# The last integer shift of the vector engine's exponential tiles moves to GpSimd, with a new tile table

## The chip, the cores and the metric

The program runs on one core of one Trainium2 chip. A core has five engines, each with an instruction queue of its own that it works off strictly in order: TensorE (PE in the profile; its weight loads are shown as PEld), VectorE (DVE), ScalarE (ACT), GpSimd (POOL) and SyncE (SP, which here only issues DMAs). They share the on-chip memory SBUF; TensorE writes its products to PSUM, eight banks of 512 float32 columns by 128 partitions. The engines wait for one another through semaphores. The metric is the device time of one execution in microseconds (us).

## The reference

One transformer block in parallel form on x of shape 1 x 2048 x 512 in bf16: the layer-normed input goes through attention and through a feed-forward part, and both are added to x.

```python
def _A_ref(x, wq, wk, wv, wo):                 # 32 query heads of 16, one shared key/value head
    ...
    scores = jnp.einsum("bhqd,bkd->bhqk", q, k) * (Dh ** -0.5)
    p = _softmax(scores, axis=-1)
    o = jnp.einsum("bhqk,bkd->bhqd", p, v)
    ...
def _B_ref(x, w1, b1, w2, b2):                 # 512 -> 1792 -> 512
    h = _gelu(jnp.einsum("bsd,df->bsf", x, w1) + b1)
    return jnp.einsum("bsf,fd->bsd", h, w2) + b2
xn = _layernorm(x, axis=-1)
return x + _A_ref(xn, A_wq, A_wk, A_wv, A_wo) + _B_ref(xn, B_w1, B_b1, B_w2, B_b2)
```

The softmax has 32 x 2048 x 2048 exponentials, some 134 million. They are what the kernel is built around.

## The kernel before

**Tiles and units.** The exponentials are cut into 2048 tiles of 128 keys by 512 queries of one head. Four heads make a group, a group has 64 tiles, and there are 32 groups (8 per block of 512 queries, four blocks). Three tiles in a row form a unit; there are 683 units. `scores(u)` (L890) makes the scores of a unit with three matmuls of 32 rows each into three PSUM banks. Two sets of three banks take turns, so the scores of unit u+2 can only be written when everything of unit u has been read out of its banks.

**Two ways to an exponential.** A table, the string `DTAB`, has one character per unit and says which of its tiles are E tiles and which are D tiles.

- The E tiles of a unit are done by one activation on ScalarE, `exp(u)` (L913), PSUM to the SBUF tile `E`. Each needs one product with V.
- A D tile is done on VectorE. `p1` (L944) reads the scores from PSUM, adds an offset, clamps from below and writes int16 into `Dt`: read as the bits of a bf16 this is a straight-line approximation of the exponential. To mend it, five copies of the tile are used, shifted by -26, 0, 26, 51 and 77 (`SPL_K`); each is multiplied with a copy of V scaled by a weight of its own (`SPL_C`), and TensorE sums the five products. A D tile therefore needs five products with V (`pv_mm`, L949), an E tile one.

**Batches and shifts.** D tiles are gathered into batches of one to six (a character of `CLOSE` ends a batch). `close_batch` makes the shifted copies on VectorE, SBUF to SBUF in int16 (L977), with the three steps of `SPL_STEPS`, each given as destination buffer, source buffer, number of buffers, constant:

```python
SPL_STEPS = ((1, 0, 1, 26), (2, 0, 2, 51), (0, 0, 1, -26))
```

The first writes buffer 1 from buffer 0; the second writes buffers 2 and 3 from buffers 0 and 1 in one instruction; the third shifts buffer 0 in place, when the product with the unshifted tile and both earlier steps have read it. So a batch of n tiles takes three instructions, over n, 2n and n tiles, and the products that use each copy become ready behind it.

**The rest.** VectorE also evacuates the products' sums (`o_evac`, L989), normalises them (L1016, both inputs in SBUF), moves the results of the side matmuls out of PSUM (L1052, L1065, L1080, L1126) and squares the queries (L1053, both inputs in SBUF). ScalarE also runs the GELU (L1092). TensorE runs, between the scores and the products with V, all side matmuls (projections, feed-forward; `mm4`, L605). GpSimd has only the set-up: constants, masks and the scaled copies of V (L847), all within the first 29 us.

**Order.** The instruction order of every engine is written before the program is emitted, by `Prog.schedule`. It plays the program through with a cost (`occ`) and a latency (`lat`) for each operation and gives each engine, when it becomes free, the ready operation with the earliest due time (`rdy + allow`; `P1_ALLOW = -20` puts a ready `p1` ahead of all else on VectorE). `emit` then writes each engine's list with the semaphore waits that the dependences need. At run time nothing is reordered.

Of the kernel before, what the change touches and what calls it, by code (L numbers as in the profile page):

```python
# [15 lines left out]
SPL_K = (-26, 0, 26, 51, 77)  # L16
SPL_C = (0.39453125, 0.349609375, 0.298828125, 0.259765625, 0.2265625)
SPL_NB = 4
SPL_STEPS = ((1, 0, 1, 26), (2, 0, 2, 51), (0, 0, 1, -26))
SPL_D = -107.78043958019079  # L20
SPL_MIN = 64.0
SWITCH = 0.1
# [10 lines left out]
EV_ALLOW = -2.0  # L33
# [10 lines left out]
LAL = 30.0  # L44
LCO = 0.0
PRO_FROM = 2.0
TBL = 1
DMASK = {".": (), "0": (0,), "2": (2,), "a": (0, 1), "b": (1, 2), "x": (0, 1, 2),
         "o": (0,), "t": (2,), "A": (0, 1), "B": (1, 2), "X": (0, 1, 2)}
CLOSE = "otABX"  # L50
DTAB = "t00o0.202.oot.0.ot2b...2ot20.20.t.o222200...o20t.202.2o.2o.2.o0220.o0o...t22o0.ot2..22t..00t0o2t.0.0t2022..0.0t2oa.222o.....o2to2o.2.2o.ott2.222t.20...00o00..oo.020oo.222oo.2to.aBxAoo22ot2.2..o.t0to2t22toot..200oo02...to.2ttt02t0000..00..222ot0t0.2.02o222.222.oo.o.22tt0t0.o..o002..2to002.t202.t.2tt0.002o0.0o.to.o.tt2...2.tot0202o20.o0..2..202o2.22o.02o..00o00.20t2A..2o22tt.2.22.0o.0.20.t2tt002.2t0.o0..2.t022.ot2.t.t2222t.0.22t0o2.0t222t...2ottt2..2t0to0.o0t..t2.to..00o2.2t.2o0o2.2..0.o..2o..o.to2.o0.02toXxxA.22t2.2t2.000o20.02.2t.2o2a..t2.t0t.00o00222.o0t0t.o22222t2.00..2.0o.2ot.o22.t2o.t.20o2t220t2...022ott020...t2.0o00.2o20.20o2.t.o2t22to.o..o222t.02022.200too..20t..2ooo.."
Y_ALLOW = 8.0
H_ALLOW = 5.0
YT_ALLOW = (3,3,3,3)
# [31 lines left out]

class _Op:
    __slots__ = ("eng", "fn", "deps", "sdeps", "stream", "amt", "need", "ticket", "waits", "clock", "occ", "lat",
                 "allow", "kind", "tag", "nun", "outs", "rel", "pm", "rdy", "start", "end", "vis", "idx", "done", "due", "real")


class Prog:
# [16 lines left out]
        self.fill_deps = []  # L109
        self.log = []  # L110

    def add(self, eng, fn, r=(), w=(), acc=None, dma=None, occ=0.1, lat=0.15, allow=1.0, kind=None, tag=None, after=(), due=None):
        op = _Op()
        op.eng, op.fn = eng, fn
        op.stream = dma or eng
        op.amt = 16 if dma else 1
# [89 lines left out]
    def schedule(self):  # L206
# [30 lines left out]
        opened = None  # L237
        s_seen = False
        vleft = sum(op.kind == "v" for op in ops)
        left = sum(1 for o in ops)  # L240
        nfill = 0
        while left:
# [11 lines left out]
            if e == "pe":  # L254
# [53 lines left out]
                if op is None or isinstance(op, float):  # L308
                    free["pe"] = t + 0.03 if op is None else op
                    continue  # L310
                visit = visit + 1 if op.kind in ("pv", "side") and mode == "col" else 1
            else:
                op = min(cand, key=self.due)
                if e == "dve" and op.kind != "p1":
                    nx = min([o.rdy for o in ready[e] if o.kind == "p1"] + [t + 9.0])
                    if 1e-6 < nx - t < min(P_WAIT, op.occ / 2):
                        free["dve"] = nx
                        continue
# [39 lines left out]
            else:  # L358
                op.start = t
                op.end = t + op.occ  # L360
                op.vis = op.end + op.lat
            if e == "pe":
                while op.start > wend:
                    slow = 1.0 if area > HAM_T * WIN else 2.0
                    ncold += slow > 1
                    self.log.append((wend - WIN, area / WIN, slow))
                    area, wend = 0.0, wend + WIN
                pend = op.start + op.occ * slow
# [52 lines left out]
    def emit(self):  # L421
# [4 lines left out]
        for op in self.ops:  # L426
            kn = known[op.eng]
            op.waits = []
            for o in sorted(op.deps, key=lambda o: -len(o.clock)):
                if kn.get(o.stream, 0) >= o.ticket:  # L430
                    continue
                op.waits.append((o.real, o.stream, o.ticket))
                for s, t in o.clock.items():
                    if kn.get(s, 0) < t:
                        kn[s] = t
# [31 lines left out]
def bass_parallel_sum__grouped_kv_mqa__dense_activation_gelu__prompt_kernel(  # L467
# [34 lines left out]
    with ExitStack() as es:  # L502
# [81 lines left out]
        def vcost(n, mode=1):  # L584
            return n / 0.96e3 / mode + 0.065
# [368 lines left out]
        def close_batch():  # L954
# [19 lines left out]
            for o, i, nb, k in SPL_STEPS:  # L974
                def keys(b):
                    return [(("D", base[b + m > 0] + q), b + m) for m in range(nb) for q in range(n)]
                dve(lambda e, d=view(o, nb), q=view(i, nb), k=k: e.tensor_scalar(d, q, float(k), None, ALU.add),  # L977
                    r=keys(i) if i != o else (), w=keys(o), n=nb * n * TBW, mode=4, allow=1.0, kind="post")
# [8 lines left out]
        def o_evac(gg):  # L987
# [59 lines left out]
        def q_pack(tb, p, gls=(0, 1)):  # L1047
            s = p % 2
            for d in range(DT):
# [233 lines left out]
```

## Time and profile before

| | |
|---|---|
| time, median of 3 runs | 767.58 us (767.33 to 769.11) |
| span of the profiled execution, first to last instruction | 765.7 us |
| busy: PE / DVE / ACT / POOL | 747.8 / 751.4 / 750.6 / 16.5 us |
| exponentials on ScalarE (L913) | 679 instructions, 699.8 us busy: 184 of three tiles, 487 of two, 8 of one |
| `p1` on VectorE (L944) | 498 instructions for 514 tiles, 339.9 us busy |
| shifts on VectorE (L977) | 663 instructions (221 batches), 348.5 us busy |
| products with V (L949) | 2570 of D tiles, 1534 of E tiles |

The time around the span (start and end of the execution) is not in the profile; the median of the three runs stands 1.9 us above the span of the profiled execution, whose own time is not given apart from it. The duration of a VectorE or ScalarE instruction in a row is longer than the distance to the start of the next one when two follow each other without a wait: the next starts before the last one's results have landed. Costs below are therefore distances from start to start of neighbours in the timeline, where they can be had.

### The profile page before, as it was taken

The page shows a single profiled execution, that of the slowest core. Times are in us where ns is not written, and L with a number is a line of the kernel's source. Part 1 is how long each engine was busy: PE and PEld are TensorE (multiplying, and loading weights), DVE is VectorE, ACT ScalarE, POOL GpSimd, SP SyncE. Part 2 cuts the span into 40 slices and gives each one's busy share as a digit, 9 for nine tenths or more (in the row PEclk, how much of TensorE's full clock was granted, in tenths as well). Part 3 has the DMA queues.
Part 4 walks back from the last instruction along what each step waited for, and adds up shares of the span by engine and source line. Part 5 has one row for each costly group of instructions (what it writes and reads, how often), then busy time and mean ns, then how long its engine had stood idle before and what let it go on. Part 6 is the DMA issues. An engine that isn't in the chain of part 4 may idle for free.

```text
span 765.7 us, 21236 instructions
## 1 busy us (share of the span) xinstructions
PE 747.8 (98%) x8948; PEld 231.4 (30%) x8950; DVE 751.4 (98%) x1403; ACT 750.6 (98%) x745; POOL 16.5 (2%) x55
## 2 busy tenths in 40 slices
PE   7999999999999999999999999999999999999998
PEld 5323222332232322222232223232233233322223
DVE  8899999999999999999999999999999999999997
ACT  8999999999999999999999999999999999999995
POOL 5300000000000000000000000000000000000000
PEclk8999999999999999999999999999999999999999
DMA  9100101000001010101100010100100101010001
GB/s 314 55 14 12 29 16 24 11 19 16 12 17 37 5 42 23 24 23 25 27 11 25 26 26 23 31 9 20 30 13 13 27 30 37 16 45 17 21 17 37
DMA packets 32072, 23.29 MB, mean 30 GB/s; under 512 B 16369, under 2 KB 27498, under 8 KB 31978
## 3 DMA queue, kind: packets, MB, share of 16 engines
q1 hardware_dynamic: 30922, 21.90, 11.1%
q8 instruction: 71, 1.16, 0.7%
q14 instruction: 23, 0.19, 0.1%
q10 hardware_dynamic: 1056, 0.03, 0.1%
HBM read 13.08 MB, written 2.35 MB: 20 GB/s over the span
## 4 chain that ended last, share of the span: by engine, by line
PE 42%; ACT 41%; DVE 14%; issue 1%; DMA 1%; DVEq 0%; SPq 0%; POOL 0%
ACT E L913 40%; PE pAll L949 20%; PE pAll L890 13%; PE pAll L605 8%; DVE Dt L944 6%; DVE Dt L977 6%; DVE x_sb L1080 1%; DMA x_sb<-in_A_x_dram 1%; PE pAll L599 1%; PE pAll L743 0%; DVE Of L989 0%; ACT xnT L748 0%; DVE ub L1080 0%; DVE qp L1052 0%; DVE stats L692 0%
## 5 line engine op out<-in xcount | busy, mean ns | idle before, releaser
L913 ACT ACTIVATE E<-pAll 128x1024 bf16<-128x1024 f32 (+1 forms) x679 | 699.8, 1272 | 1.4 <-PE pAll L890 0.5
L949 PE MATMUL pAll<-Dt,V 128*32 128x512 bf16 x2570 | 400.0, 384 | 1.0 <-DVE Of L989 0.7
L977 DVE TENSOR_SCALAR Dt<-Dt 128x1024 int16<-128x1024 int16 (+7 forms) x663 | 348.5, 559 | 0.6
L944 DVE TENSOR_SCALAR Dt<-pAll 128x512 int16<-128x512 f32 (+2 forms) x498 | 339.9, 695 | 1.7 <-PE pAll L890 1.3
L949 PE MATMUL pAll<-E,V 128*32 128x512 bf16 x1534 | 284.4, 385 | 0.5 <-DVE Of L989 0.3
L890 PE MATMUL pAll<-QT,KT 32*128 32x512 bf16 x2048 | 267.2, 384 | 5.0 <-ACT E L913 2.0
L890 PEld LDWEIGHTS pAll<-QT,KT 32*128 32x128 bf16 x2048 | 66.8, 91 | 279.5 <-ACT E L913 250.7
L949 PEld LDWEIGHTS pAll<-Dt,V 128*32 128x32 bf16 x2570 | 105.5, 94 | 120.2 <-issue 69.8
L605 PE MATMUL pAll<-xnT,w_sb 128*32 128x512 bf16 x896 | 113.2, 382 | 1.4 <-DVE x_sb L1080 1.1
L949 PEld LDWEIGHTS pAll<-E,V 128*32 128x32 bf16 x1534 | 67.5, 94 | 58.4 <-issue 43.0
L605 PE MATMUL pAll<-w_sb,x_sb 128*32 128x512 bf16 x448 | 74.0, 382 | 0.0
L605 PE MATMUL pAll<-w_sb,ub 128*32 128x512 bf16 x448 | 66.2, 382 | 0.0
L605 PE MATMUL pAll<-wop,oTp 128*32 128x512 bf16 x256 | 55.5, 382 | 0.0
L605 PEld LDWEIGHTS pAll<-xnT,w_sb 128*32 128x32 bf16 x896 | 29.5, 95 | 23.9 <-issue 9.1
L605 PE MATMUL pAll<-xnT,wq_sb 128*32 128x512 bf16 x256 | 21.1, 384 | 0.0
L989 DVE COPY Of<-pAll 128x512 f32<-128x512 f32 x31 | 21.0, 678 | 0.0
L1080 DVE TENSOR_SCALAR x_sb<-pAll,b1T 128x512 bf16<-128x512 f32 x28 | 20.7, 740 | 0.1
L1080 DVE TENSOR_SCALAR ub<-pAll,b1T 128x512 bf16<-128x512 f32 x28 | 20.7, 738 | 0.1
L605 PEld LDWEIGHTS pAll<-w_sb,x_sb 128*32 128x32 bf16 x448 | 18.4, 95 | 6.7 <-issue 4.5
L1244 PE MATMUL pAll<-xnT,zeros 128*32 128x512 bf16 x204 | 19.3, 382 | 0.0
L605 PE MATMUL pAll<-b2row,ones 128*32 128x512 bf16 x64 | 18.8, 382 | 0.0
L605 PEld LDWEIGHTS pAll<-w_sb,ub 128*32 128x32 bf16 x448 | 16.9, 94 | 5.9 <-issue 4.1
(118 smaller groups left out, 227.4 us busy)
## 6 DMA issues: line engine op xcount, KB each, us to landing
OfP<-Of SPq DMA_DIRECT2D x124, 32.0 KB, 2.0
rbP<-rden_rows SPq DMA_DIRECT2D x124, 32.0 KB, 1.9
w_sb<-in_B_w_dram SPq DMA_DIRECT2D x2, 1792.0 KB, 12.7
x_sb<-in_A_x_dram SPq DMA_DIRECT2D x8, 256.0 KB, 4.8
x_sb<-in_A_x_dram SPq DMA_DIRECT2D x16, 128.0 KB, 2.1
QT<-qp SPq DMA_DIRECT2D x124, 16.0 KB, 1.8
out_dram<-x_sb SPq DMA_DIRECT2D x12, 128.0 KB, 1.8
wq_sb<-in_A_wq_dram SPq DMA_DIRECT2D x1, 512.0 KB, 6.6
```

The source lines that it names most:

```text
L599: return add("pe", lambda e: e.matmul(o, l, rh, start=start, stop=stop, **kw), r, w, occ=occ, lat=0.23, allow=allow, **ak)
L605: add("pe", lambda e, c=c, j=j: e.matmul(o[c, :], l[:, c], rh, start=start, stop=stop, tile_position=(0, 32 * j)), r, [(k, j) for k in w] ...
L890: ins = e.matmul(o, l, rh, start=True, stop=True, tile_position=(q0, 0))
L913: o = act(lambda e: e.activation(E[:, s0:s0 + na, :], bank(b0, na).rearrange("p (a n) -> p a n", a=na), ACT.Exp, scale=LN2 / 128.0), w=[B( ...
L944: return dve(lambda e: e.tensor_scalar(Dt[:, s:s + n, :], bank(bk, n).rearrange("p (a n) -> p a n", a=n), float(127 * 128) + SPL_D, SPL_MI ...
L949: add("pe", lambda e, a, b: e.matmul(pO[32 * j:32 * j + 32, :], V1[:, v, kt, :], rhs, start=a, stop=b, tile_position=(0, 32 * j)), r=r + [ ...
L977: dve(lambda e, d=view(o, nb), q=view(i, nb), k=k: e.tensor_scalar(d, q, float(k), None, ALU.add), r=keys(i) if i != o else (), w=keys(o), ...
L989: dve(lambda e: e.tensor_copy(Of[:, i, :], pO), w=["O", ("Of", i)], allow=0.0)
L1080: dve(lambda e: e.tensor_scalar(ubs[tb % 2][:, ft, :], pM, b1T[:, ft:ft + 1], None, ALU.add), r=["b1T"], w=M4 + [ukey(tb, ft)], n=TBW + 57 ...
L1244: pr.filler = lambda e, j, o: e.matmul((pO if o else pM)[32 * j:32 * j + 32, :], zeros[:, 0:32], xnT[:, 0, 0:TBW], start=not o, stop=not o ...
```

## The change

- `SPL_STEPS` loses its third step. In its place `close_batch` adds, for each tile of the batch, one instruction on GpSimd that works on the tile in place: `tensor_scalar` with two operations, times 1.0 and plus -26.0. The product with that copy follows each tile's own instruction. Nothing of the arithmetic changes.
- The planner is told that a GpSimd shift takes 0.55 us and is seen 0.2 us later (`GS_OCC`, `GS_LAT`), and that it excludes VectorE's SBUF work: operations marked `two=True` (the shifts, L1016, L1053) don't start while a GpSimd shift runs (`lock`), and a GpSimd shift doesn't start while one of them runs, nor in the last 0.35 us of another VectorE operation (`GS_MIN`).
- So that the order holds at run time, each GpSimd shift also waits for the VectorE operation that stands ahead of the last marked one (`gate`). It may then be issued while that marked one still runs.
- A GpSimd shift that has been ready for 1 us (`GS_LATE`) while VectorE is free and no `p1` is ready is offered to VectorE, as a shift of one tile.
- `DTAB` is replaced. What the two tables hold, counted with the rules of `DMASK` and `CLOSE`:

| | before | after |
|---|---|---|
| D tiles | 514 | 539 |
| E tiles | 1534 | 1509 |
| batches | 221 | 276 |
| batches of 1 / 2 / 3 / 4 / 5 / 6 tiles | 80 / 58 / 40 / 22 / 16 / 5 | 133 / 70 / 42 / 20 / 6 / 5 |
| units with 0 / 1 / 2 / 3 D tiles | 185 / 486 / 8 / 4 | 188 / 458 / 30 / 7 |

```diff
--- before.py
+++ after.py
@@ -16,7 +16,8 @@
 SPL_K = (-26, 0, 26, 51, 77)
 SPL_C = (0.39453125, 0.349609375, 0.298828125, 0.259765625, 0.2265625)
 SPL_NB = 4
-SPL_STEPS = ((1, 0, 1, 26), (2, 0, 2, 51), (0, 0, 1, -26))
+SPL_STEPS = ((1, 0, 1, 26), (2, 0, 2, 51))
+SPL_LAST = -26.0
 SPL_D = -107.78043958019079
 SPL_MIN = 64.0
 SWITCH = 0.1
@@ -44,11 +45,16 @@
 LAL = 30.0
 LCO = 0.0
 PRO_FROM = 2.0
+GS_OCC = 0.55
+GS_LAT = 0.2
+GS_MIN = 0.35
+GS_LATE = 1.0
+GS_DUE = 1.0
 TBL = 1
 DMASK = {".": (), "0": (0,), "2": (2,), "a": (0, 1), "b": (1, 2), "x": (0, 1, 2),
          "o": (0,), "t": (2,), "A": (0, 1), "B": (1, 2), "X": (0, 1, 2)}
 CLOSE = "otABX"
-DTAB = "t00..."
+DTAB = "ot...."
 Y_ALLOW = 8.0
 H_ALLOW = 5.0
 YT_ALLOW = (3,3,3,3)
@@ -86,7 +92,8 @@
 
 class _Op:
     __slots__ = ("eng", "fn", "deps", "sdeps", "stream", "amt", "need", "ticket", "waits", "clock", "occ", "lat",
-                 "allow", "kind", "tag", "nun", "outs", "rel", "pm", "rdy", "start", "end", "vis", "idx", "done", "due", "real")
+                 "allow", "kind", "tag", "nun", "outs", "rel", "pm", "rdy", "start", "end", "vis", "idx", "done", "due", "real",
+                 "two", "alt", "gate")
 
 
 class Prog:
@@ -109,8 +116,10 @@
         self.fill_deps = []
         self.log = []
 
-    def add(self, eng, fn, r=(), w=(), acc=None, dma=None, occ=0.1, lat=0.15, allow=1.0, kind=None, tag=None, after=(), due=None):
+    def add(self, eng, fn, r=(), w=(), acc=None, dma=None, occ=0.1, lat=0.15, allow=1.0, kind=None, tag=None, after=(), due=None,
+            two=False, alt=None):
         op = _Op()
+        op.two, op.alt, op.gate = two, alt, None
         op.eng, op.fn = eng, fn
         op.stream = dma or eng
         op.amt = 16 if dma else 1
@@ -237,6 +246,8 @@
         opened = None
         s_seen = False
         vleft = sum(op.kind == "v" for op in ops)
+        two_end = win_end = lock = 0.0
+        dprev = gate = None
         left = sum(1 for o in ops)
         nfill = 0
         while left:
@@ -309,8 +320,29 @@
                     free["pe"] = t + 0.03 if op is None else op
                     continue
                 visit = visit + 1 if op.kind in ("pv", "side") and mode == "col" else 1
+            elif e == "pool" and ready[e][0].kind == "gs":
+                if two_end > t or 0 < win_end - t < GS_MIN:
+                    free["pool"] = max(two_end, win_end) + 1e-4
+                    continue
+                op = min(cand, key=self.due)
+                op.gate = gate
             else:
+                if e == "dve" and s_seen:
+                    if lock > t:
+                        c1 = [o for o in cand if not o.two]
+                        if not c1:
+                            free["dve"] = min([lock] + [o.rdy for o in ready[e] if not o.two])
+                            continue
+                        cand = c1
+                    elif not any(o.kind == "p1" for o in cand):
+                        late = [o for o in ready["pool"] if o.kind == "gs" and o.rdy + GS_LATE <= t]
+                        if late:
+                            cand = cand + [min(late, key=self.due)]
                 op = min(cand, key=self.due)
+                if op.eng != e:
+                    ready["pool"].remove(op)
+                    ready["dve"].append(op)
+                    op.eng, op.stream, op.occ, op.lat, op.two, op.kind = "dve", "dve", op.alt[0], op.alt[1], True, "post"
                 if e == "dve" and op.kind != "p1":
                     nx = min([o.rdy for o in ready[e] if o.kind == "p1"] + [t + 9.0])
                     if 1e-6 < nx - t < min(P_WAIT, op.occ / 2):
@@ -359,6 +391,16 @@
                 op.start = t
                 op.end = t + op.occ
                 op.vis = op.end + op.lat
+                if e == "dve":
+                    if op.two:
+                        two_end, gate = op.end, dprev
+                    else:
+                        win_end = op.end
+                    dprev = op
+                elif op.kind == "gs":
+                    lock = op.end
+                    if gate is not None:
+                        gate.need = True
             if e == "pe":
                 while op.start > wend:
                     slow = 1.0 if area > HAM_T * WIN else 2.0
@@ -426,6 +468,8 @@
         for op in self.ops:
             kn = known[op.eng]
             op.waits = []
+            if getattr(op, "gate", None) is not None and op.gate not in op.deps:
+                op.deps.append(op.gate)
             for o in sorted(op.deps, key=lambda o: -len(o.clock)):
                 if kn.get(o.stream, 0) >= o.ticket:
                     continue
@@ -975,10 +1019,17 @@
                 def keys(b):
                     return [(("D", base[b + m > 0] + q), b + m) for m in range(nb) for q in range(n)]
                 dve(lambda e, d=view(o, nb), q=view(i, nb), k=k: e.tensor_scalar(d, q, float(k), None, ALU.add),
-                    r=keys(i) if i != o else (), w=keys(o), n=nb * n * TBW, mode=4, allow=1.0, kind="post")
+                    r=keys(i), w=keys(o), n=nb * n * TBW, mode=4, allow=1.0, kind="post", two=True)
                 for m in range(nb):
                     have[o + m] = have[i + m] + k
                 sums(range(o, o + nb))
+            v = 1 + SPL_K.index(int(SPL_LAST))
+            for q, (t, _) in enumerate(batch):
+                gg, kt, j = tile_of(t)
+                d, key = Dt[:, base[0] + q, :], (("D", base[0] + q), 0)
+                add("pool", lambda e, d=d: e.tensor_scalar(d, d, 1.0, SPL_LAST, ALU.mult, ALU.add), w=[key],
+                    occ=GS_OCC, lat=GS_LAT, allow=GS_DUE, kind="gs", alt=(vcost(TBW, 4), 0.16))
+                pv_mm(gg, j, v, kt, d.bitcast(bf), [key])
             del batch[:]
 
         onorm = {}
@@ -1014,7 +1065,7 @@
                 n = 64 if end else P
                 keys = [(k, s, hh, j) for k in ("OfP", "rbP") for hh in range(h + 1) for j in range(HG)]
                 onorm[gg - h] = onorm[gg] = dve(lambda e: e.tensor_tensor(oTp[0:n, sl, :], OfP[0:n, s, :], rbP[0:n, s, :], ALU.mult),
-                                                r=keys, w=[("oTp", sl)] + pre.pop(sl, []), allow=3.0)
+                                                r=keys, w=[("oTp", sl)] + pre.pop(sl, []), allow=3.0, two=True)
 
         def o_norm_last(gg):
             RB1 = [[("rbP", 0, h, j) for j in range(HG)] for h in range(2)]
@@ -1051,7 +1102,7 @@
                    r=["wq"] + tr(4 * tb, 4 * tb + 4), w=[B(7)], allow=QP_ALLOW)
             dve(lambda e: e.tensor_copy(qp[:, s, :], pM), w=M4 + [("qp", s)], allow=EV_ALLOW)
             dve(lambda e: e.tensor_tensor(sqq[:, s, :], qp[:, s, :], qp[:, s, :], ALU.mult), r=[("qp", s)],
-                w=[("sq", s)], mode=2, allow=EV_ALLOW)
+                w=[("sq", s)], mode=2, allow=EV_ALLOW, two=True)
             for gl in gls:
                 for j in range(HG):
                     r0 = 64 * gl + Dh * j
```

More of the change, by code (lines that the diff above doesn't have):

```diff
@@ L50 @@
 CLOSE = "otABX"
-DTAB = "t00o0.202.oot.0.ot2b...2ot20.20.t.o222200...o20t.202.2o.2o.2.o0220.o0o...t22o0.ot2..22t..00t0o2t.0.0t2022..0.0t2oa.222o.....o2to2o.2.2o.ott2.222t.20...00o00..oo.020oo.222oo.2to.aBxAoo22ot2.2..o.t0to2t22toot..200oo02...to.2ttt02t0000..00..222ot0t0.2.02o222.222.oo.o.22tt0t0.o..o002..2to002.t202.t.2tt0.002o0.0o.to.o.tt2...2.tot0202o20.o0..2..202o2.22o.02o..00o00.20t2A..2o22tt.2.22.0o.0.20.t2tt002.2t0.o0..2.t022.ot2.t.t2222t.0.22t0o2.0t222t...2ottt2..2t0to0.o0t..t2.to..00o2.2t.2o0o2.2..0.o..2o..o.to2.o0.02toXxxA.22t2.2t2.000o20.02.2t.2o2a..t2.t0t.00o00222.o0t0t.o22222t2.00..2.0o.2ot.o22.t2o.t.20o2t220t2...022ott020...t2.0o00.2o20.20o2.t.o2t22to.o..o222t.02022.200too..20t..2ooo.."
+DTAB = "ot.02.02o22.o.o00A.o..2.t202ot.t2.2tBo.2.2o.t22o0.oA.oo..ot.02o.2o2tot.0o...20ooo2.oott.20o.ttot2o0t...ta.bo.00o20o..2t...oo2.tt0t.t.2.02a2t.202.2t.0.2..0B..o0o.B.tt0.oo.22tob20a.XXott0oo.20t0020..o22o2ot0to.Bo.o0002.o.2.oooa.2t.t00..o0..o22to2.tto0.20B.t.22o.0o0bt.t2.0t22..02tt.2.atot2to.2t..bt.2.20t0.0.2ao2t.2200.20.oo.0to..o22o2t.2o.t20t.o.Xo.0.t...2ttt.2oooo2o.0.t.b.oo00.02t2.22..t.2ooo.2B220o0t.2..o20.2.0t2.20tt22o..0.t2t20tt.202otoot..t0tt.t.2t2t0Xot2...2tt2..02.t02.2o00o2..to.o0..2.2.b22.t.t.tt0o0XXxA.ot.t2o.2t0o0ot00o0t...a0oto.to0o22t.0.2oo.0to2.2tt0ott..0ot0o.B2t.2...A22t020.to.o.t22o2o2.o2t0t02.2oto..t0ta.2t.2B.0t.t22b...t.a.0tt.to2o.t.b00o..to.0A.tt2to0.oo.oo..2."
 Y_ALLOW = 8.0
```

## The prediction

> **What bounds the kernel now.** I read the page's busy line first, then its chain, then the waits, the groups of instructions with shapes kept apart, and last the timeline where GpSimd and VectorE overlap.
>
> ```profile
> PE 747.8 (98%) x8948; PEld 231.4 (30%) x8950; DVE 751.4 (98%) x1403; ACT 750.6 (98%) x745; POOL 16.5 (2%) x55
> PE 42%; ACT 41%; DVE 14%; issue 1%; DMA 1%; DVEq 0%; SPq 0%; POOL 0%
> ```
>
> VectorE and ScalarE are both full, GpSimd is empty. PE's 98% is no bound of its own: the end of a matmul is modelled, and the list of waits shows its queue held up by ScalarE.
>
> ```profile
> PEld pAll L890 <- ACT E L913: 250.7, 606, 0.8
> PEld pAll L890 <- DVE Dt L944: 19.7, 47, 1.1
> PEld pAll L949 <- DVE Dt L977: 19.1, 70, 0.6
> ```
>
> The first line (total us, times, longest) says that the score matmuls mostly wait for ScalarE to read out a bank; VectorE is the releaser far less often. In the chain in order of time there are long stretches of ScalarE alone:
>
> ```profile
> 331.15 64.28 ACT E L913 x62
> 418.80 76.65 ACT E L913 x74
> 609.59 88.35 ACT E L913 x86
> ```
>
> Elsewhere, from 200 to 331 us above all, the chain alternates between PE and VectorE's `p1` and shifts. So the two engines are balanced, and only a change that relieves both shortens the kernel.
>
> ```profile
> L913 ACT ACTIVATE E<-pAll 128x1024 bf16<-128x1024 f32 x487 | 483.6, 1161 | 1.2 <-PE pAll L890 0.5
> L913 ACT ACTIVATE E<-pAll 128x1536 bf16<-128x1536 f32 x184 | 281.5, 1592 | 0.2
> L913 ACT ACTIVATE E<-pAll 128x512 bf16<-128x512 f32 x8 | 5.6, 695 | 0.0
> L944 DVE TENSOR_SCALAR Dt<-pAll 128x512 int16<-128x512 f32 x486 | 323.7, 678 | 1.6 <-PE pAll L890 1.3
> L977 DVE TENSOR_SCALAR Dt<-Dt 128x1024 int16<-128x1024 int16 x196 | 78.5, 414 | 0.3
> L977 DVE TENSOR_SCALAR Dt<-Dt 128x512 int16<-128x512 int16 x160 | 43.4, 279 | 0.1
> ```
>
> From start to start in the timeline, back to back, these take less than their durations: an exponential 0.904 us (two tiles), 1.330 (three), 0.494 (one); a `p1` 0.60, which is 0.066 + 0.533 a tile; a shift 0.20 for one tile, 0.33 for two, 0.60 for four, which is 0.066 + 0.133 a tile.
>
> **ScalarE: fewer tiles.** Before: 487 x 0.904 + 184 x 1.330 + 8 x 0.494 = 688.9 us. After (units with one, none, two D tiles): 458 x 0.904 + 188 x 1.330 + 30 x 0.494 = 678.9. That is -10.0 us. Against it: after the eight one-tile exponentials ScalarE now loses 1.65 us in all beyond 0.494 each, 0.21 apiece, since the bank set is held by two `p1` for 1.13 us. The 22 more cost 22 x 0.21 = 4.5 us; between 0 (VectorE has them done early) and 22 x 0.35 = 7.7 (the worst of the eight). The three more units without any ScalarE tile I cost at nothing, because neighbouring units' exponentials cover their 1.67 us of `p1`; without that cover they add at most 3 x 1.67 - 3 x 0.904 = 2.3 us.
>
> **VectorE: what leaves.** Shifts before: 514 tiles x 4 passes x 0.133 + 663 x 0.066 = 318 us. After: 539 x 3 x 0.133 + 552 x 0.066 = 252. `p1`: 25 tiles x 0.533, less 3 x 0.066 for three fewer instructions, +13. Sum -53: VectorE's work falls from 751 to 698 us if every GpSimd shift stays on GpSimd. One that the planner gives back costs 0.20; if a fifth go back (108), +21.
>
> **PE: five products instead of one.** 25 x 4 = 100 more matmuls of 32 columns; four run beside each other in 0.216 us (distance between groups in the timeline), so 100/4 x 0.216 = 5.4 us. They lie in the 250 us that the score queue waits for ScalarE; without that cover they cost the 5.4. No DMA is added or moved, and POOL's queue holds nothing else after 29 us.
>
> **GpSimd: what one shift takes.** No row shows this form. Bounds from the rows of the set-up, again from start to start:
>
> ```profile
> 22.34 4.65 POOL L847 TENSOR_SCALAR V<-oTp 128x256 bf16<-128x256 f32 x5 [5.15 <-DVE oTp L841]
> 27.51 0.52 POOL L857 MEMSET wol<- 128x512 bf16 x1
> 4.47 0.41 POOL L646 COPY oTp<-wvk 128x256 bf16<-128x256 bf16 x1
> 4.83 0.23 POOL L695 TENSOR_SCALAR nm<-sm 128x1 f32<-128x1 f32 x1
> 5.69 0.19 POOL L655 TENSOR_SCALAR isc<-mrow 128x1 f32<-128x1 f32 x1
> ```
>
> Low end: a memset of 512, 0.47 us, which reads nothing. Reading and writing: the copy of 256 takes 0.36, that is 0.14 + 0.86 ns an element, so 0.58 us for 512. High end: the one-operation tensor_scalar of 256, 0.94 us each, 0.14 + 3.1 ns an element, so 1.7 us for 512. By opcode the last is nearest. I still take 0.58, for two reasons. At one column the two-operation form (L655, next start 0.13 us on) is quicker than the one-operation ones (L695, L710: 0.15 to 0.19), so it seems to run another way. And the planner's costs of the set-up agree with their rows (L847 booked 0.93, shown 0.94; L658 1.35 and 1.37; L646 0.35 and 0.36), and for this shift it books 0.55.
>
> The Trainium skill's "GPSIMD Engine Reference" (section 3.1) puts a body of at most two operations at 1.03 cycles an element and the best tight loop at 1.8, with 0.77 us for 512 elements; no row here shows either, and by 0.77 the sum would end as the second rival's does.
>
> **GpSimd and VectorE together.** The planner puts a GpSimd shift under a `p1` or another PSUM reader (0.60 us) and keeps VectorE's shifts out until it ends. There are 495 `p1` and some 140 other such operations, 635 windows for at most 539 shifts: enough. What sticks out at the end of a window is lost to VectorE. A shift that waits for its own batch's second step starts about 0.15 us into the window and sticks out 0.58 + 0.15 - 0.60 = 0.13; one released by an older step sticks out nothing. I take 0.08: 539 x 0.08 = 43 us. VectorE: 698 + 43 = 741, some 10 us under its present load. That this is close is the main doubt.
>
> What a collision costs, the timeline shows once:
>
> ```profile
> 25.35 0.93 DVE L977 TENSOR_SCALAR Dt<-Dt 128x512 int16<-128x512 int16 x2
> ```
>
> Two VectorE shifts, of one and two tiles, begin inside the fourth L847. To the next start they take 0.38 and 0.47 us, 0.18 and 0.14 more than elsewhere; the GpSimd ones keep their distance of 0.93. So that collision cost about 0.16 us a shift.
>
> By the Trainium skill's "SBUF — State Buffer" (section "Who interferes with whom") the two engines' common port pair is an exclusive lock for the whole instruction and the later one fully blocks; by that the first shift would have stood 0.7 us, so this trace does not show the rule in full.
>
> **The new waits.** Each GpSimd shift waits for VectorE twice over, and its product stands in PE's queue: if the shift is late, all of PE behind it is late, the next scores too. PE has about 0.5 us to spare in an exponential of 0.9 us (a score matmul takes 0.38 by its row, L890), so a shift up to 0.4 us late costs nothing and every 0.1 beyond delays ScalarE by 0.1.
>
> **The sum.** -10.0 (ScalarE's tiles) + 4.5 (one-tile units) = -5.5. VectorE's relief takes back part of the 9.6 us that ScalarE now stands beyond its minimum after two- and three-tile exponentials before the tail (12.6 less 3.0 for the wait at the tail): I take 2 of them, between 0 and 5. New stalls from late shifts: 0.5, between 0 and the rivals below. -7 us: 765.7 becomes 758.7, and with the 1.9 around it the median 767.6 becomes 760.6. With the bounds of these terms (0 to 7.7 for one-tile units, 0 to 2.3 for units without an exponential, 0 to 5 for relief) it lies between 752.5 and 767.6; I give 754 to 765.
>
> **The rivals.**
>
> 1. *VectorE stays the bound.* What sticks out and what goes back to VectorE (43 + 21 us) eat the relief of 53, VectorE stands at 762 and the shorter ScalarE work is filled with waiting: 766 to 770. For it: VectorE has 14 us of idle time now. Against it: the overhang of 0.08 would have to hold beside a fifth given back.
>
> 2. *A GpSimd shift is longer than its window, and VectorE's next shift stands until it ends* (the other side). The place is the first marked VectorE operation behind each GpSimd shift. VectorE may grow from 741 to about 754 before it costs time: 13 us over 539 shifts, 0.024 us each, so from about 0.60 us a shift it decides. At 0.70 it is 539 x 0.10 = 54 us more than that: 760.6 + 54 = 815. If a collision costs only the 0.16 seen above and half the shifts collide, 270 x 0.16 = 43, less the 43 already booked: nothing is lost. Between these a shift of 0.65 to 0.70 gives 770 to 815. At the one-operation row's 1.7, GpSimd alone needs 539 x 1.7 = 916 us, and the time passes 940. For it: the only wide tensor_scalar rows on GpSimd. Against it: the copy and memset rows, and the 0.16. The skill's lock rule is the mild form of this rival.
>
> 3. *The work hardly moves.* The planner offers to VectorE what is 1 us late; if it takes nearly all, GpSimd stays empty, VectorE pays 539 x 0.20 = 107 us for the 66 it saved on shifts, plus 13: 751 + 54, a time near 820. Against it: `p1` has the right of way and there are more windows than shifts.
>
> **How the numbers follow.** A measurement of this kernel tells 0.3%, 2.3 us, from no change. The forecast (faster) 0.52; rival 1 0.10, half of it within 0.3%, the rest split evenly; rival 2 0.35, nearly half of it up to 815, the rest above; rival 3 0.03. Faster 0.54, same 0.06, slower 0.40. For 8 in 10 the range must reach into rival 2: 752 to 830. The forecast's own range is 754 to 765.
>
> **What would show it.** Right: L944 with 495 instructions, L977 with 552 plus what went back, on POOL about 430 to 539 tensor_scalars 0.5 to 0.65 us apart at the closest; ACT's L913 near 690 us busy; DVE below 745; few waits on POOL in the list for PE. Rival 2: POOL spans of 0.7 us or more, DVE shifts of 0.5 us and more for one or two tiles, PE waiting for POOL or for DVE L977 by tens of us. Rival 1: DVE at 98% again. Rival 3: L977 near 1000. Most likely to make the forecast wrong is GpSimd's price, which no row shows.

## The result, and the profile after

The changed kernel takes 776.21 us (median of four runs, 776.06 to 777.18), the one before 767.46: 1.0109 times as long, 95% interval 1.0095 to 1.0124. It is slower by 8.7 us, where the prediction had it faster by 7. The span of its profiled execution is 774.4 us, 8.7 more than before.

The page's busy line and chain of the changed kernel:

```profile
PE 752.7 (97%) x9036; PEld 235.8 (30%) x9038; DVE 736.1 (95%) x1392; ACT 746.4 (96%) x742; POOL 319.5 (41%) x492
...
PE 50%; DVE 16%; ACT 2%; POOL 2%; issue 1%; DVEq 0%
```

Both engines that were full have less to do: VectorE 736 us against 751, ScalarE 746 against 751. The span grew all the same, so both wait more. The shares of this chain add up to 71%: it is followed back only to 216 us. In that part ScalarE is 2% of the span; before, it had stretches of 64 to 88 us of its own there. PE has taken its place. The groups that answer to those shown before, and the new ones (shapes kept apart; busy, mean ns, idle before and who ended it):

```profile
L957 ACT ACTIVATE E<-pAll 128x1024 bf16<-128x1024 f32 x459 | 447.6, 1069 | 11.6 <-PE pAll L934 9.9 <-PE pAll L993 0.2
L957 ACT ACTIVATE E<-pAll 128x1536 bf16<-128x1536 f32 x187 | 274.3, 1496 | 3.1 <-PE pAll L934 2.3
L957 ACT ACTIVATE E<-pAll 128x512 bf16<-128x512 f32 x30 | 20.2, 675 | 0.0
L988 DVE TENSOR_SCALAR Dt<-pAll 128x512 int16<-128x512 f32 x460 | 305.5, 678 | 22.0 <-PE pAll L934 20.8 <-PE pAll L643 0.4
L1030 POOL TENSOR_SCALAR Dt<-Dt 128x512 int16<-128x512 int16 x437 | 303.2, 694 | 434.5 <-DVE Dt L1021 239.7 <-PE pAll L993 88.4 <-PE pAll L934 31.5
L1021 DVE TENSOR_SCALAR Dt<-Dt 128x1024 int16<-128x1024 int16 x203 | 86.5, 439 | 0.2
L1021 DVE TENSOR_SCALAR Dt<-Dt 128x512 int16<-128x512 int16 x133 | 38.3, 299 | 0.1
L1030 DVE TENSOR_SCALAR Dt<-Dt 128x512 int16<-128x512 int16 x102 | 25.6, 282 | 0.0
```

Of the 539 last shifts 437 run on GpSimd and 102 on VectorE, given back by the planner. A GpSimd shift takes 0.69 us on average. VectorE's own shifts got longer (one tile 299 ns against 279, two tiles 439 against 414), and `p1` (L988) and the exponentials (L957) now sit idle for scores (L934), 20.8 and some 12 us. The list of waits says what PE stands for (total us, times, longest):

```profile
PEld pAll L934 <- ACT E L957: 210.9, 522, 0.8
PEld pAll L934 <- DVE Dt L988: 33.9, 82, 0.6
PEld pAll L993 <- POOL Dt L1030: 18.2, 46, 3.3
PE pAll L993 <- POOL Dt L1030: 4.5, 5, 2.8
```

The scores wait for ScalarE 40 us less than before; PE's queue stands 18.2 us for GpSimd at the weight loads. The 4.5 us at the matmuls are not to be added: the longest wait of both rows ends at the same moment, 589.29 us. The worst place is at 586 us (timeline of the changed kernel; start, length, engine, idle before and who ended it):

```profile
582.50 8.14 POOL L1030 TENSOR_SCALAR Dt<-Dt 128x512 int16<-128x512 int16 x7 [0.67 <-DVE Dt L1030]
586.41 2.35 DVE L1021 TENSOR_SCALAR Dt<-Dt 128x1536 int16<-128x1536 int16 x4
589.29 1.04 PE L993 MATMUL pAll<-Dt,V 128*32 128x512 bf16 x6 [2.78 <-POOL Dt L1030]
591.35 0.69 DVE L988 TENSOR_SCALAR Dt<-pAll 128x512 int16<-128x512 f32 x1 [2.59 <-PE pAll L934]
```

Seven GpSimd shifts take 8.1 us there. One of them begins at 585.93 and ends 3.31 us later; in that time VectorE runs six SBUF shifts back to back (586.01 to 588.76). PE stands 2.8 us for it, the scores behind it come late, and VectorE and ScalarE wait for them. Behind the stall TensorE's granted clock is half for 3.4 us (busy us and instructions of PE, its weight loads, VectorE, ScalarE and GpSimd; then clock and DMA):

```profile
586.00:589.10 3.10, 0.52 (x5) 0.02 (x4) 2.76 (x7) 2.48 (x3) 3.10 (x1) 0.99 0.00 0
589.10:592.50 3.40, 3.21 (x23) 0.70 (x23) 0.69 (x1) 1.02 (x1) 1.38 (x3) 0.51 0.00 0
```

Three scores take 0.61 us in that stretch (at 590.69) instead of 0.39. At half speed 3.4 us cost PE at most 1.7 us, an estimate from these rows. The kernel before has no such stretch between 15 us and its end.

### The profile page after: what moved, and what is told of

The parts are those of the page before. It is cut to its first block, busy times and chain, and to the rows that moved or that the text cites. A ratio compares the mean times of both kernels' runs of the same rounds, so it can differ in the third digit from the quotient of the medians.

```text
span 774.4 us, 21977 instructions
## 1 busy us (share of the span) xinstructions
PE 752.7 (97%) x9036; PEld 235.8 (30%) x9038; DVE 736.1 (95%) x1392; ACT 746.4 (96%) x742; POOL 319.5 (41%) x492
## 4 chain that ended last, share of the span: by engine, by line
PE 50%; DVE 16%; ACT 2%; POOL 2%; issue 1%; DVEq 0%
PE pAll L993 25%; PE pAll L934 16%; PE pAll L649 9%; DVE Dt L988 7%; DVE Dt L1021 6%; ACT E L957 2%; POOL Dt L1030 2%; PE pAll L1295 1%; DVE Dt L1030 1%; DVE x_sb L1131 0%; DVE qp L1103 0%; DVE Of L1040 0%; DVE oTp L1067 0%; DVE ub L1131 0%; DVE sqq L1104 0%
## 5 line engine op out<-in xcount | busy, mean ns | idle before, releaser
L957 ACT ACTIVATE E<-pAll 128x1024 bf16<-128x1024 f32 (+1 forms) x676 | 695.6, 1169 | 14.6 <-PE pAll L934 12.1
L1030 POOL TENSOR_SCALAR Dt<-Dt 128x512 int16<-128x512 int16 x437 | 303.2, 694 | 434.5 <-DVE Dt L1021 239.7
L993 PE MATMUL pAll<-Dt,V 128*32 128x512 bf16 x2695 | 436.3, 385 | 5.7 <-POOL Dt L1030 4.5
L988 DVE TENSOR_SCALAR Dt<-pAll 128x512 int16<-128x512 f32 (+2 forms) x496 | 351.6, 724 | 25.6 <-PE pAll L934 24.4
L1021 DVE TENSOR_SCALAR Dt<-Dt 128x1024 int16<-128x1024 int16 (+6 forms) x552 | 290.8, 558 | 0.9
L993 PE MATMUL pAll<-E,V 128*32 128x512 bf16 x1509 | 288.0, 385 | 0.7 <-DVE Of L1040 0.6
L934 PE MATMUL pAll<-QT,KT 32*128 32x512 bf16 x2048 | 267.6, 385 | 3.7 <-ACT E L957 1.0
L993 PEld LDWEIGHTS pAll<-Dt,V 128*32 128x32 bf16 x2695 | 116.4, 95 | 143.3 <-issue 74.0
L934 PEld LDWEIGHTS pAll<-QT,KT 32*128 32x128 bf16 x2048 | 67.2, 91 | 270.0 <-ACT E L957 210.9
L649 PE MATMUL pAll<-xnT,w_sb 128*32 128x512 bf16 x896 | 124.2, 383 | 1.3 <-DVE qp L1103 0.6
L649 PE MATMUL pAll<-w_sb,x_sb 128*32 128x512 bf16 x448 | 70.6, 383 | 0.0
L1030 DVE TENSOR_SCALAR Dt<-Dt 128x512 int16<-128x512 int16 x102 | 25.6, 282 | 0.0
```

Source lines behind the costliest of these rows:

```text
L649: add("pe", lambda e, c=c, j=j: e.matmul(o[c, :], l[:, c], rh, start=start, stop=stop, tile_position=(0, 32 * j)), r, [(k, j) for k in w] ...
L934: ins = e.matmul(o, l, rh, start=True, stop=True, tile_position=(q0, 0))
L957: o = act(lambda e: e.activation(E[:, s0:s0 + na, :], bank(b0, na).rearrange("p (a n) -> p a n", a=na), ACT.Exp, scale=LN2 / 128.0), w=[B( ...
L988: return dve(lambda e: e.tensor_scalar(Dt[:, s:s + n, :], bank(bk, n).rearrange("p (a n) -> p a n", a=n), float(127 * 128) + SPL_D, SPL_MI ...
L993: add("pe", lambda e, a, b: e.matmul(pO[32 * j:32 * j + 32, :], V1[:, v, kt, :], rhs, start=a, stop=b, tile_position=(0, 32 * j)), r=r + [ ...
L1030: add("pool", lambda e, d=d: e.tensor_scalar(d, d, 1.0, SPL_LAST, ALU.mult, ALU.add), w=[key], occ=GS_OCC, lat=GS_LAT, allow=GS_DUE, kind= ...
```

## The experiments

The theory after this reading: GpSimd's shift costs more than the 0.55 us it is booked at, in two ways. It is late for its product, and PE, which works off a fixed list, stands; and it keeps VectorE's shifts from SBUF while it reads and writes there itself (below: it holds the port). The rival: the order itself is the longer one, whatever GpSimd takes.

**What a shift and a meeting cost.** A kernel of its own, on tiles of 128x512 int16 (`two`: the change's form, `one`: one operation, `cpy`: copy; `shift` and `wide`: VectorE, one and four tiles; `p1`: a PSUM read; each phase is what GpSimd does, then what VectorE does):

```diff
+PH = [([(two, 8)], []), ([(one, 4)], []), ([(cpy, 4)], []),
+      ([], [(shift, 8), (wide, 4), (p1, 6)]),
+      ([(two, 12)], [(p1, 12)]), ([(two, 12)], [(shift, 24)]),
+      ([(two, 12)], [(wide, 10)]), ([(two, 12)], [(mix, 20)]), ([(one, 6)], [(shift, 24)])]
```

> A kernel of its own that leaves the whole computation out (its output is zeros) and only runs, in nine phases with a wait of both engines between them, GpSimd and VectorE on separate tiles of 128x512 int16: GpSimd alone with the two-operation shift (8), the one-operation shift (4), a copy (4); VectorE alone with a shift of one tile (8), of four tiles (4), a PSUM read as in p1 (6); then both at once: 12 two-operation shifts against 12 PSUM reads, against 24 one-tile shifts, against 10 four-tile shifts, against 20 in turn; last 6 one-operation shifts against 24 one-tile shifts. Price theory (GpSimd takes longer than the 0.55 us booked, and blocks): two-operation 0.70 us from start to start, one-operation 1.5 us or more; against PSUM reads nothing changes on either side; against shifts each VectorE shift that meets a GpSimd one stands until that ends, 0.3 us or more on average. Mild theory (collisions cost 0.16 us, as the one in the trace before): VectorE shifts get 0.1 to 0.2 us longer, GpSimd ones less than 0.1.

Timelines of this kernel, GpSimd alone, then both engines:

```profile
13.12 5.41 POOL L26 TENSOR_SCALAR G<-G 128x512 int16<-128x512 int16 x8 [0.33 <-DVEq L56]
18.78 6.15 POOL L27 TENSOR_SCALAR G<-G 128x512 int16<-128x512 int16 x4 [0.25 <-DVEq L56]
25.16 2.28 POOL L28 COPY G<-G 128x512 int16<-128x512 int16 x4 [0.23 <-DVEq L56]
...
35.42 8.13 POOL L26 TENSOR_SCALAR G<-G 128x512 int16<-128x512 int16 x12 [7.97 <-DVEq L56]
35.42 7.27 DVE L31 TENSOR_SCALAR D<-ps 128x512 int16<-128x512 f32 x12 [0.19 <-DVEq L56]
...
43.64 9.94 DVE L29 TENSOR_SCALAR D<-D 128x512 int16<-128x512 int16 x24 [0.95 <-POOLq L56]
43.80 9.63 POOL L26 TENSOR_SCALAR G<-G 128x512 int16<-128x512 int16 x12 [0.25 <-POOLq L56]
...
53.77 11.47 POOL L26 TENSOR_SCALAR G<-G 128x512 int16<-128x512 int16 x12 [0.34 <-DVEq L56]
53.77 10.31 DVE L30 TENSOR_SCALAR W<-W 128x2048 int16<-128x2048 int16 x10 [0.20 <-DVEq L56]
...
74.74 8.61 DVE L29 TENSOR_SCALAR D<-D 128x512 int16<-128x512 int16 x24 [1.33 <-POOLq L56]
74.91 10.46 POOL L27 TENSOR_SCALAR G<-G 128x512 int16<-128x512 int16 x6 [0.25 <-POOLq L56]
```

Alone, the two-operation shift takes 0.62 us and the next begins 0.68 after it ((5.41 - 0.62) / 7); the one-operation form 1.49 and 1.55; the copy 0.61 and 0.56. Beside PSUM reads neither side changes (0.68 and 0.60). Against shifts the two take turns. With one-tile shifts a round is one GpSimd shift and two VectorE ones in 0.82 us, 0.42 more than two shifts (0.20 each) take alone; with four-tile shifts one and one in 1.02, again 0.42 more than 0.60. So a meeting costs VectorE 0.42 us, two thirds of the GpSimd shift's 0.62, and the GpSimd shift itself then takes 0.76 or 0.95 us. Beside the one-operation form (last phase) nine of the 24 VectorE shifts stand 0.41 us each, two to a GpSimd shift, and the ones between them pass at 0.20. This decides between the two theories of that run: dearer than 0.16, cheaper than standing to the end. The Trainium skill's "SBUF — State Buffer" (section "Who interferes with whom") has the pair locked for the whole instruction; here the loser stood 0.42 of 0.62 us. The Trainium skill's "GPSIMD Engine Reference" (section 3.1) has 1.03 cycles an element for such a body, which is 0.44 us at the page's 1.2 GHz, an estimate that fits the hold, not the duration.

**The same order with a cheap GpSimd shift.** Order and waits of all instructions stay; the shift works on 2 of 512 columns.

```diff
-add("pool", lambda e, d=d: e.tensor_scalar(d, d, 1.0, SPL_LAST, ALU.mult, ALU.add), w=[key],
+add("pool", lambda e, d=d[:, 0:2]: e.tensor_scalar(d, d, 1.0, SPL_LAST, ALU.mult, ALU.add), w=[key],
```

> The changed kernel with the same order of all instructions and the same waits, but each GpSimd shift works on 2 of its 512 columns (the other columns stay unshifted, so this part of the computation is left out). GpSimd's price and its hold on the port are gone, the order and the waits stay. If price and collisions cost the time, it falls to 764 us or below, under the kernel before. If the order itself is the longer one (PE's products, one- and two-tile units, windows kept for GpSimd), it stays at 769 to 774 us.

761.23 us, 0.9919 of before (0.9903 to 0.9936). The rival falls: the order with the new table is 6 us shorter than before, and GpSimd's cost eats 15. But the edit also narrowed the 102 shifts that VectorE had been given back. With only the GpSimd ones narrowed:

```diff
+def gs_fn(e, d=d, n=len(pr.ops)):
+    if gs_ops[n].eng == "pool":
+        return e.tensor_scalar(d[:, 0:2], d[:, 0:2], 1.0, SPL_LAST, ALU.mult, ALU.add)
+    return e.tensor_scalar(d, d, 1.0, SPL_LAST, ALU.mult, ALU.add)
```

> As the first narrow run (order and waits of the changed kernel, GpSimd shifts on 2 of 512 columns, the rest left unshifted), but the 102 shifts that the planner gave back to VectorE stay whole. The first narrow run had narrowed these too and so spared VectorE some 102 x 0.08 to 0.13 us. If that saving was in idle time, 761 to 763 us again; if VectorE's own load matters as much as the port, 765 to 770, and the share of the port and of GpSimd's time in the 15 us is smaller by as much.

762.75 us, 0.9939 (0.9922 to 0.9955). So GpSimd's own cost, beyond a shift of 0.19 us, is 13.5 us. With the cheap shift ScalarE is back in the chain, and PE hardly stands for GpSimd; the first narrow kernel's page, whose chain goes back to the start, and its waits:

```profile
PE 61%; ACT 32%; DVE 6%; DMA 0%; issue 0%; DVEq 0%; SPq 0%
...
PEld pAll L993 <- POOL Dt L1030: 2.0, 9, 0.2
```

**GpSimd's time without most of the port.** The one-operation form on 158 columns takes 0.61 us, as long as the change's shift, and moves a third of the data.

```diff
-e.tensor_scalar(d, d, 1.0, SPL_LAST, ALU.mult, ALU.add)
+e.tensor_scalar(d[:, 0:158], d[:, 0:158], SPL_LAST, None, ALU.add)
```

> Same order and waits as the changed kernel; each GpSimd shift is the slow one-operation form on 158 of 512 columns (the rest is left unshifted, so that part of the computation is left out). By the two-port run's 1.49 us for 512 columns this takes GpSimd about as long as the changed kernel's shift (0.6 us), but moves a third of the data through the port. If late products (PE's queue standing for GpSimd) are the cost, it stays at 773 to 777 us. If the port is, it falls to 761 to 766.

767.00 us, but again with VectorE's 102 narrowed too. With those whole:

> As the run with GpSimd shifts of 158 columns in the one-operation form (as long as the changed kernel's, a third of the data), but with the 102 of VectorE whole. GpSimd's time without most of the port: 767 to 769 us if VectorE's saving was in idle time, 771 to 774 if not.

772.02 us: 9.3 over the narrow one, 4.2 under the changed kernel. Here VectorE's spared 9 us (102 x 0.09) were worth 5 us, although VectorE stands idle for some 40 us in both runs; in the narrow kernels the spared 13 us (102 x 0.13) were worth 1.5. The port is not wholly gone: from start to start VectorE's shifts still lose some 6 us here, 2 in the narrow kernel and 14 in the changed one.

**The port without the late product.** The shift is whole but writes a scratch tile, and the product reads the unshifted tile without waiting for it. The scratch has two tiles, so each shift also waits for the one two before it; VectorE stands 0.5 us for that.

```diff
-e.tensor_scalar(d, d, 1.0, SPL_LAST, ALU.mult, ALU.add)
+e.tensor_scalar(scrG[:, hG[0], :], d, 1.0, SPL_LAST, ALU.mult, ALU.add)
...
+pr.ops[-1].deps = [o for o in pr.ops[-1].deps if o is not gs] + [o for o in gs.deps if o.eng == "dve"]
```

> Same order as the changed kernel; the GpSimd shift is whole, with its full time on GpSimd and on the port, but it writes a scratch tile, and the product reads the unshifted tile and does not wait for it (so the shift is left out of the result). If late products are the cost, it falls to 762 to 766 us. If VectorE's collisions on the port are, it stays at 772 to 777.

769.76 us: 7.0 over the narrow one, 6.4 under the changed kernel. Each of the two cuts splits the same 13.5 us: late products cost between 6.4 and 9.3 us, the port between 4.2 and 7.0. Since the 9.3 still holds some of the port, the split by this cut is likely the nearer one. Neither expectation held alone; both causes are there.

**Without the gate.** The wait of each GpSimd shift for the operation ahead of the last marked one is left out; those that the data need stay.

```diff
-if getattr(op, "gate", None) is not None and op.gate not in op.deps:
-    op.deps.append(op.gate)
```

> The changed kernel, whole, without the wait of each GpSimd shift for the operation ahead of the last marked VectorE one (the waits that the data need stay). If GpSimd is mostly late, starting as soon as the data are there helps: 770 to 775 us. If the wait keeps it out of VectorE's way, more collisions: 778 to 785.

791.08 us, 1.0306 (1.0289 to 1.0323). VectorE's shifts, measured from start to start against their unhindered distance, lose some 27 us, 14 in the changed kernel, 3 in the first narrow one and 2 in the kernel before. The gate works; it is worth 15 us.

**One part of the change alone.** The shift on GpSimd with the old table, and the new table with all shifts on VectorE (in both the only edit is the line of `DTAB`).

> The change with the old table (514 D tiles, 221 batches): the shift alone. If relieving VectorE of 66 us of shifts is worth something by itself, 762 to 768 us. If a table only fits the order it was made with, and the moved shift throws that order over, 785 us or more.

> The kernel before with the new table (539 D tiles, 276 batches), all shifts on VectorE: the table alone. By VectorE's work, 25 more tiles (25 x 1.07 us) and 165 more shift instructions (x 0.066) are 38 us on a VectorE that was 98% busy: 800 us; up to 830 if the order falls apart too. If ScalarE's 10 us were the bound, 758 to 768.

794.88 and 826.26 us, one run each. Neither part gains alone: with the old table, the moved shift, which frees VectorE of up to 83 us (514 x 0.133 + 221 x 0.066), is 28 us slower than before. The second is near VectorE's sum (805) plus a disturbed order. In both the planner makes another order out of the mixed parts, so these two do not say what GpSimd costs in the changed kernel's.

**Giving PE time.** If the product is late, let PE do other work first.

```diff
+while j + 1 < len(order) and order[j + 1].start < op.start + LATE_BY and op not in order[j + 1].deps:
+    j += 1
+order.insert(j, order.pop(i))
```

> The changed kernel, whole; only PE's list differs: each product that waits for a GpSimd shift stands up to 0.6 us of planned time later, behind work that does not need it. If PE standing for late shifts costs the 6 us that the run without product waits took off (776.2 to 769.8), a good part comes back: 770 to 774 us. If the port alone holds the kernel back, it stays at 775 to 777.

801.34 us. It tells nothing of late products, since it breaks something else. The scores' queue stood 61.8 us at issue, against 23.2; why, no run shows. What it shows is that PE's list has little play.

**Giving shifts back to VectorE at the same place of the order**, the two at 585.2 and 585.9 us; then all that stand fourth or later in an unbroken planned run (21); then also those that in the trace of that run let PE stand over 0.18 us or a VectorE shift over 0.2 (53); then with limits of 0.09 (95). The cut shows the second; the others name the shifts by planned time or by number.

```diff
+if run >= 4:
+    op.eng = op.stream = "dve"
+    op.gate = None
```

> The changed kernel, whole, in its order, but the two GpSimd shifts at 585.2 and 585.9 us (the last two of a run of five, one of which stood 3.3 us behind a train of VectorE shifts while PE stood 2.8 us for it) are done by VectorE at the same place of the order, 0.20 us each. If that one stall costs what the slip against the planned order shows there (3.7 us), 772 to 774 us. If PE's time there was spare, 776.

> The same for all 21 GpSimd shifts that the planner put fourth or later in an unbroken run on GpSimd (0.55 us apart in the plan, 0.70 on the chip, so 0.45 us late or more at the fourth). VectorE pays 21 x 0.20 = 4 us of which it has 29 idle. If late products in such runs are the larger part of the 6 us that waiting for products costs, 769 to 772 us; if lateness is spread over all shifts, 773 to 775.

> The changed kernel, whole, in its order, with 53 of the 437 GpSimd shifts done by VectorE at the same place: the 21 of the last run, and those 32 that in its trace let PE stand for over 0.18 us or a VectorE shift for over 0.2 us. VectorE pays 32 x 0.20 = 6 us more. If what is left of the loss sits at these few meetings, 764 to 768 us, level with or under the kernel before; if giving back only moves the waits to the next shift (VectorE's own load takes over), 769 to 773.

> The same with 95 given back (limits of 0.09 us for both). VectorE pays 74 x 0.20 = 15 us more than in the run with 21, of some 25 idle. If the meetings are the loss, 762 to 767 us; if VectorE's load takes over, worse than the run with 53.

772.93, 770.89, 769.71 and 772.38 us; against before 1.0063, 1.0037, 1.0024 (1.0014 to 1.0035) and 1.0058. The single stall at 586 us cost 3.3, the halved clock behind it included: with these two given back the clock is full there. With 53 given back PE stands 3.8 us for GpSimd at weight loads, against 18.2, and yet 7 us over the narrow kernel remain. VectorE's load seems to take their place. The waits with 53 given back (total us, times, longest):

```profile
PEld pAll L939 <- DVE Dt L993: 48.6, 116, 0.7
...
PEld pAll L998 <- POOL Dt L1035: 3.8, 17, 0.3
```

and with 95 given back:

```profile
PEld pAll L939 <- DVE Dt L993: 56.2, 133, 0.8
...
PEld pAll L998 <- POOL Dt L1035: 2.6, 11, 0.4
```

The scores wait 49 and 56 us for `p1`, 34 in the changed kernel, and the run with 95 is slower than the one with 53, as was expected if VectorE's load takes over. None of these four mixes beats the kernel before.

**Why one shift stood 3.3 us.** Two more benches, the computation left out: VectorE shifts with signals, in place, each waiting for the one before it, and in the train seen at 586 us; then that train with its start moved by 17 ns from trial to trial.

```diff
+PH = [([(twoi, 12)], [(shift, 24)]), ([(two, 12)], [(count(shifti), 24)]), ([(twoi, 12)], [(count(shifti), 24)]),
+      ([(twoi, 12)], [(inpl, 24)]), ([(twoi, 12)], [(chain, 24)]), ([(twoi, 12)], [(p1, 2), (train, 12)])]
...
+PH = [([(twoi, 3)], [(lead(w), 1), (train2, 6)]) for w in range(16, 512, 16)]
```

> Like the first two-port run (the computation is left out, the output is zeros): 12 two-operation GpSimd shifts against VectorE shifts of several kinds, in six phases. Only GpSimd signals a semaphore; only VectorE does; both do; VectorE works in place; each VectorE shift waits for the one before it; last two PSUM reads and two trains of shifts of 1, 1, 3, 2, 6 and 4 tiles, each signalling, as in the changed kernel at 586 us where one GpSimd shift took 3.3 us. If a signal decides who gets the port, GpSimd shifts of 1 us and more are seen where VectorE signals, and of 0.76 us elsewhere. If the two always take turns, 0.76 us against one-tile shifts everywhere, and at most 0.62 + 0.80 us in the trains.

> Again a kernel of its own without the computation (output zeros): 31 trials, each with three GpSimd shifts against a PSUM read on VectorE whose width goes from 16 to 496 columns in steps of 16 (17 ns) and behind it a train of six VectorE shifts (1, 1, 3, 2, 6, 4 tiles, the first two in place with two operations). So the moment at which the train begins moves by 0.5 us against GpSimd's requests for the port. If a close finish between the two lets VectorE's whole train go first, some trials show a GpSimd shift of 2.5 to 3.3 us, as in the changed kernel at 586 us. If the two always take turns, none is over 1.3 us.

In both the engines always took turns; the longest GpSimd shift was 1.20 and 1.01 us. This line of the first gives the durations of all its 72 (min/median/max ns):

```profile
L29 POOL TENSOR_SCALAR G<-G x72: 620/739/1204, 24.1 to 87.2; 128x512 int16<-128x512 int16 x72
```

In the kernel whole trains pass: at 586 us, and without the gate in several places, where a GpSimd shift stood 1.4 to 3.3 us through two to six VectorE shifts. The shift at 586 us begins 0.08 us after the end of the one before it, as the others of its run do, so its waits had been met and it stood while it ran. What lets a train pass in the kernel and not in the bench stays open.

## Why the prediction was wrong

- **ScalarE's tiles, -10.0.** Right at the floor: 459 x 0.904 + 187 x 1.330 + 30 x 0.494 = 678.5 us, 10.4 below before. What ScalarE stands beyond that floor, from start to start and with the wait at the tail, went from 14.3 to 34.0 us, and 19.7 - 10.4 = 9.3 is the loss, near the 8.7 of the span.
- **VectorE's relief, -2.0, and new stalls, +0.5.** These are the two terms that failed. What ScalarE stands after two- and three-tile exponentials before the tail, of which 2 us were to vanish, went from 9.6 to 21.8 us. With GpSimd made cheap (762.75 us) it is 9.2, so the 12 us more are GpSimd's doing. The steps that led to these terms follow.
- **One-tile units, +4.5.** Mis-sized, within its bound of 7.7: the 30 lose 9.3 us, 0.31 each for the 0.21 taken, 7.6 more than before. In the two narrow kernels they still lose 7.9 and 8.2: most of this is the table's, not GpSimd's.
- **VectorE's work, 698 to 741.** Near in sum: 736 us busy, 552 shifts as counted, 496 `p1` for 495, 102 given back (a fifth, as bounded). The parts are others: some 14 us at meetings and 20 for the 102, where 43 were booked for what sticks out, so the sum is in part luck. (The shifts before come to 317 us, not 318.)
- **GpSimd's shift, 0.58 us.** The first failed step. It takes 0.62 and, one behind the other in the kernel, repeats every 0.70. The choice of path was right (the one-operation form takes 1.49); the copy's row gave the wrong spacing, and the planner's 0.55, which the prediction leaned on, is lower than either. The prediction put the point from which the price decides at 0.60. The time, 776 us, lies between the 770 and 815 of rival 2, but not by that rival's sum: VectorE's work never reached its limit of 754 us. The room of 13 us below that limit was none; at 736 us the port cost 4.2 to 7.0. The late products are not in that sum at all, so that 776 falls into its band is in part luck.
- **The collision, 0.16 us.** Wrong size: 0.42 in the bench. It is not the slow form that made the one in the trace cheaper, since beside that form too a VectorE shift stood 0.41. The one in the trace met tiles of 256 elements, float32 to bf16, instead of 512 in int16; whether that is the reason, no run shows.
- **"A shift up to 0.4 us late costs nothing", stalls of 0.5 us.** The second failed step. Late products cost 6.4 to 9.3 us. Counted by the prediction's own rule, with only what exceeds 0.4 us in each of the 46 waits of weight loads for GpSimd, the trace of the changed kernel gives 4.7 us, 2.9 of them at 586 us. So half or more of the error is that so little lateness was expected, the one long stall above all; the rule itself falls short by 1.7 to 4.6 us. How shorter waits cost time is argued only: between two scores PE's list is packed with products and side matmuls, and a product that comes late moves the scores behind it, as at 586 us.
- **The sum.** With GpSimd made cheap the order takes 762.75 us, near the 760.6 forecast. The order was worth what was forecast; the price of GpSimd's shift was set too low.
- **Rivals 1 and 3.** VectorE is idle 38 us and not the bound of the changed kernel; 437 shifts did move.

## What to carry to other kernels

When work moves from a full engine to an empty one, the price on the new engine has to be measured in the form, the size and the spacing in which it will run: here an order made for 0.55 us met shifts that repeat every 0.70, hold VectorE up by 0.42 at a meeting and come late, and 5 us of gain became 9 us of loss. Whether the same change planned with 0.70 would gain was not run. Idle time summed over a run is no slack, on PE as on VectorE: ask what stands behind the product or the shift that comes late. And a change made of two parts that were planned together can tell little when one part is run without the other.

## What the runs showed that was not expected

The same add costs GpSimd 0.62 us as times-one-plus-constant and 1.49 us as a single operation. GpSimd's shift holds VectorE's SBUF shifts up for 0.42 us, less than it takes, and not at all under PSUM reads. When VectorE's shifts and PSUM reads alternate, GpSimd's shifts cost VectorE nothing: a pair still takes 0.80 us, and GpSimd repeats every 0.80 instead of 0.68. A wait that the data do not need, the gate, saves 15 us. After one stall of PE of 2.8 us the granted clock was half for 3.4 us. And a train of VectorE shifts kept GpSimd out for 2.7 us in the kernel, which no bench repeated.
